# Feature-map attention and a gated convolution on one core: two alternating phases become one hand-ordered pipeline of 36 units

## The chip, the cores and the metric

The kernel runs on one core of one Trainium2 chip. The metric is the device time of one execution in microseconds (us). The core's engines are PE (TensorE, with its weight loads shown apart as PEld), DVE (VectorE), ACT (ScalarE), POOL (GpSimd) and SP (SyncE, which here only issues DMAs). Each works through its own queue in order and waits on semaphores for the others.

## The reference

Eight batches, eight heads, 576 tokens, head dimension 64, 128 features, all inputs float32:

```python
def phi(x):                                   # q, k: (8, 8, 576, 64); w_phi: (64, 128)
    proj = np.einsum('bhsd,df->bhsf', x, w_phi)
    proj = proj - np.max(np.abs(proj), axis=-1, keepdims=True)
    return np.concatenate([np.exp(proj), np.exp(-proj)], axis=-1)
q_p, k_p = phi(q), phi(k)
kv = np.einsum('bhsf,bhsd->bhfd', k_p, v)
z = np.sum(k_p, axis=2)
num = np.einsum('bhsf,bhfd->bhsd', q_p, kv)
den = np.einsum('bhsf,bhf->bhs', q_p, z)[..., None] + 1e-06
x = (num / den)                               # heads side by side: (8, 576, 512)
gate = sigmoid(causal depthwise conv of x, 5 taps, conv_w (5, 512))
out = (gate * (x @ w_val)) @ w_out            # (8, 576, 512)
```

## The kernel before

A batch's tokens are cut into five chunks, four of 128 and one of 64 that is padded to 128 (`CHUNKS`). Matmul operands are bf16; POOL's DMAs convert while they load. A batch passes through these steps:

- Loads (L110, L111, L119): 15 DMAs per batch from POOL, one for each chunk of q, k and v, in runs of 64 floats (256 B).
- `emit_transposes` (L136): PE transposes q and k of two heads at a time into PSUM (L142, L153), DVE copies them to QT2 and KT2 (L147 to L159).
- `emit_qmax` (L163): q is projected with tokens on the partitions (five matmuls, 640 columns) only so that DVE can take the largest magnitude per token (L171). `emit_mqrows` turns these maxima into rows (L182, L183).
- `emit_kproj` (L185): k is projected the same way into PK; DVE takes the maxima (L194), ACT writes exp(PK) and exp(-PK) to KTIL (L198, L199).
- `emit_vscale` (L201): ACT takes exp of minus and plus the k maxima (EMK, EPK, L204, L205); POOL multiplies v by them (L211) and puts them in an extra 65th column (L215). That column gives z.
- `emit_qproj` (L219): q is projected with features on the partitions into PQ; the q maxima are subtracted by matmuls with EB (L224, L226); ACT writes both exps to QTIL (L227, L228).
- KV (L388): 10 matmuls of 65 columns per head, evacuated by DVE (L248).
- `emit_num` (L253): per chunk 16 matmuls of 65 columns (L259), then DVE's reciprocal and product (RCP L268, XN L270). `emit_xtp` (L278) transposes XN on PE and copies it to XT on DVE (L283, L284): here the heads of all channels come to the partitions.
- The MLP: per 256 tokens and 128 channels four matmuls with WVAL (L292) and five with diagonal matrices of the taps, DIAG (L300), which are the convolution; tanh on ACT (L307; the sigmoid is 0.5 (1 + tanh(x/2)), with the halves folded into weights), the gated product on DVE (L310); then matmuls with WOUT (L322), a copy on ACT (L329) and the store from SP (L330).

The outer loop alternates two phases, each with its own PSUM pools. `phase_X` does transposes, maxima and k of batch i+1 together with the MLP of batch i-2, and ends with `emit_vscale`; `phase_Y` does q and KV of batch i together with NUM and XTP of batch i-1. The code gives a program order, and a scheduler then chooses the order in each engine's queue. The half-size contraction of 64 is padded: W4 holds w_phi in 64 of 128 rows and zeros in the others, so every such matmul is a full one.

Of the kernel before, what the change touches and what calls it, by code (L numbers as in the profile page):

```python
# [10 lines left out]
ALU = mybir.AluOpType  # L11

# [5 lines left out]
NF = 2 * F  # L18
DM = 512
P = 128  # L20
CHUNKS = [(0, 128), (128, 128), (256, 128), (384, 128), (512, 64)]
NCH = len(CHUNKS)
TOKPAD = 4
QCOLS = 640


class _BatchState:
    pass


@with_exitstack
def kernel(
# [11 lines left out]
    nc = tc.nc  # L44

    const = ctx.enter_context(tc.tile_pool(name="const", bufs=1))

    ident_bf = const.tile([P, P], BF16, name="ident_bf")
    make_identity(nc, ident_bf[:])
    ident_f = const.tile([P, P], FP32, name="ident_f")  # L50
    make_identity(nc, ident_f[:])
# [3 lines left out]
    nc.sync.dma_start(wtmp[D:2 * D, :], w_phi[:, :])  # L55
    W4 = const.tile([P, 2, NF], BF16, name="W4")
    nc.vector.memset(W4[:, :, :], 0.0)
    nc.vector.tensor_copy(W4[0:D, 0, 0:F], wtmp[0:D, :])
    nc.vector.tensor_scalar_mul(W4[0:D, 0, F:NF], wtmp[0:D, :], -1.0)
    nc.vector.tensor_copy(W4[D:2 * D, 1, 0:F], wtmp[D:2 * D, :])  # L60
    nc.vector.tensor_scalar_mul(W4[D:2 * D, 1, F:NF], wtmp[D:2 * D, :], -1.0)

    EB = const.tile([P, H, P], BF16, name="EB")
    for h in range(H):
        nc.vector.tensor_copy(EB[:, h, :], ident_f[:, h:h + 1].to_broadcast([P, P]))

    WVAL = const.tile([P, 4, DM], BF16, name="WVAL")
    nc.gpsimd.dma_start(WVAL[:, :, :], moe_w_val.rearrange("(dt p) j -> p dt j", p=P))
    WOUT = const.tile([P, 4, DM], BF16, name="WOUT")
    nc.gpsimd.dma_start(WOUT[:, :, :], moe_w_out.rearrange("(jt p) o -> p jt o", p=P))  # L70
    nc.vector.tensor_scalar_mul(WOUT[:, :, :], WOUT[:, :, :], 0.5)

    cw5 = const.tile([5, DM], FP32, name="cw5")
    nc.sync.dma_start(cw5[:, :], moe_conv_w[:, :])
    cwT = const.tile([P, 4, 5], FP32, name="cwT")
    with tc.tile_pool(name="ps_cw", bufs=1, space=bass.MemoryType.PSUM) as ps_cw:
        cwps = ps_cw.tile([P, 4, 5], FP32, name="cwps")
        for dt in range(4):
            nc.tensor.transpose(cwps[:, dt, :], cw5[:, dt * P:(dt + 1) * P], ident_f[0:5, 0:5])
        nc.vector.tensor_copy(cwT[:, :, :], cwps[:, :, :])  # L80
    DIAG = const.tile([P, 4, 5, P], BF16, name="DIAG")
    cwTh = const.tile([P, 4, 5], FP32, name="cwTh")
    nc.vector.tensor_scalar_mul(cwTh[:, :, :], cwT[:, :, :], 0.5)
    for dt in range(4):
        for tap in range(5):
            nc.vector.tensor_scalar_mul(DIAG[:, dt, tap, :], ident_f[:, :], cwTh[:, dt, tap:tap + 1])

    qkp = ctx.enter_context(tc.tile_pool(name="qkp", bufs=3))
    vnp = ctx.enter_context(tc.tile_pool(name="vnp", bufs=2))
    xtp = ctx.enter_context(tc.tile_pool(name="xtp", bufs=2))  # L90
    qtp = ctx.enter_context(tc.tile_pool(name="qtp", bufs=8))
    ktp = ctx.enter_context(tc.tile_pool(name="ktp", bufs=4))
    featq = ctx.enter_context(tc.tile_pool(name="featq", bufs=2))
    featk = ctx.enter_context(tc.tile_pool(name="featk", bufs=2))
    smallp = ctx.enter_context(tc.tile_pool(name="smallp", bufs=2))
    vtp = ctx.enter_context(tc.tile_pool(name="vtp", bufs=1))
    kvp = ctx.enter_context(tc.tile_pool(name="kvp", bufs=2))
    xnp = ctx.enter_context(tc.tile_pool(name="xnp", bufs=3))
    mlp_sb = ctx.enter_context(tc.tile_pool(name="mlp_sb", bufs=2))

    def load_qk(st):
        bi = st.bi
        st.QN = qkp.tile([P, NCH, H, D], BF16, name="QN")
        st.KN = qkp.tile([P, NCH, H, D], BF16, name="KN")
        nc.gpsimd.memset(st.QN[64:P, NCH - 1, :, :], 0.0)
        nc.gpsimd.memset(st.KN[64:P, NCH - 1, :, :], 0.0)
        qrb = q[bi].rearrange("h s d -> s h d")
        krb = k[bi].rearrange("h s d -> s h d")
        for c, (s0, sz) in enumerate(CHUNKS):
            nc.gpsimd.dma_start(st.QN[:sz, c, :, :], qrb[s0:s0 + sz])  # L110
            nc.gpsimd.dma_start(st.KN[:sz, c, :, :], krb[s0:s0 + sz])  # L111

    def load_v(st):
        bi = st.bi
        st.VN = vnp.tile([P, NCH, H, D], BF16, name="VN")
        nc.gpsimd.memset(st.VN[64:P, NCH - 1, :, :], 0.0)
        vrb = v[bi].rearrange("h s d -> s h d")
        for c, (s0, sz) in enumerate(CHUNKS):
            nc.gpsimd.dma_start(st.VN[:sz, c, :, :], vrb[s0:s0 + sz])  # L119

    def alloc_A(st):
        st.MQ = smallp.tile([P, H, NCH], FP32, name="MQ")
        st.MK = smallp.tile([P, H, NCH], FP32, name="MK")
        st.MQR = smallp.tile([P, S], BF16, name="MQR")
        st.KTIL = featk.tile([P, H, NCH, NF], BF16, name="KTIL")
        st.QT2 = []
        st.KT2 = []
        st.VTs = []

    def alloc_Q(st):  # L130
        st.QTIL = featq.tile([P, H, 2, QCOLS], BF16, name="QTIL")
        nc.gpsimd.memset(st.QTIL[:, :, :, S:QCOLS], 1.0)
        st.KVSB = kvp.tile([P, H, 2, D + 1], BF16, name="KVSB")
        st.XN = {}

    def emit_transposes(st, hp, psX):  # L136
        QT2 = qtp.tile([P, 640], BF16, name="QT2")
        KT2 = ktp.tile([P, 640], BF16, name="KT2")
        srcs = ((st.QN, QT2, 0), (st.KN, KT2, 1))
        T2 = psX.tile([P, 2, 128], BF16, name="T2")  # L140
        for src, dst, ti in srcs:
            nc.tensor.transpose(  # L142
                T2[:, ti, 0:P],
                src[:, 4, 2 * hp:2 * hp + 2, :].rearrange("p h d -> p (h d)"),
                ident_bf[:, :],
            )
        nc.vector.tensor_copy(QT2[:, 512:640], T2[:, 0, 0:128])  # L147
        nc.vector.tensor_copy(KT2[:, 512:640], T2[:, 1, 0:128])
        T = psX.tile([P, 2, 512], BF16, name="T", tag="T")
        for c in range(4):  # L150
            s0, sz = CHUNKS[c]
            for src, dst, ti in srcs:
                nc.tensor.transpose(  # L153
                    T[:, ti, s0:s0 + sz],
                    src[:, c, 2 * hp:2 * hp + 2, :].rearrange("p h d -> p (h d)"),
                    ident_bf[:, :],
                )
        nc.vector.tensor_copy(QT2[:, 0:512], T[:, 0, :])
        nc.vector.tensor_copy(KT2[:, 0:512], T[:, 1, :])  # L159
        st.QT2.append(QT2)  # L160
        st.KT2.append(KT2)

    def emit_qmax(st, h, psX):  # L163
        hp, h2 = h // 2, h % 2
        PQA = psX.tile([P, NCH, F], FP32, name="PQA", tag="PA", bufs=2)
        for c, (s0, sz) in enumerate(CHUNKS):
            nc.tensor.matmul(  # L167
                PQA[:, c, :], st.QT2[hp][:, s0:s0 + P], W4[:, h2, 0:F],
                start=True, stop=True,
            )  # L170
        nc.vector.tensor_reduce(  # L171
            st.MQ[:, h, :], PQA[:, :, :],
            mybir.AxisListType.X, ALU.max, apply_absolute_value=True,
        )

    def emit_mqrows(st, psX):
        MQT = psX.tile([P, 640], BF16, name="MQT", tag="T")
        MQb = smallp.tile([P, NCH, P], BF16, name="MQb")
        nc.vector.memset(MQb[:, :, :], 0.0)
        nc.vector.tensor_copy(MQb[:, :, 0:H], st.MQ[:, :, :].rearrange("p h c -> p c h"))  # L180
        for c, (s0, sz) in enumerate(CHUNKS):
            nc.tensor.transpose(MQT[:, s0:s0 + P], MQb[:, c, :], ident_bf[:, :])  # L182
        nc.vector.tensor_scalar_mul(st.MQR[:, :], MQT[:, 0:S], -1.0)  # L183

    def emit_kproj(st, h, psX):  # L185
        hp, h2 = h // 2, h % 2
        KT2 = st.KT2[hp]
        PK = psX.tile([P, NCH, F], FP32, name="PK", tag="PA", bufs=2)
        for c, (s0, sz) in enumerate(CHUNKS):
            nc.tensor.matmul(  # L190
                PK[:, c, :], KT2[:, s0:s0 + P], W4[:, h2, 0:F],
                start=True, stop=True,
            )
        nc.vector.tensor_reduce(  # L194
            st.MK[:, h, :], PK[:, :, :],
            mybir.AxisListType.X, ALU.max, apply_absolute_value=True,
        )
# [31 lines left out]

    KVBLK_PER_PASS = 7  # L230

    def emit_kv(st, h, KVPS):
        for ft in range(2):
            VT = st.VTs[ft]
            blk = h * 2 + ft
# [248 lines left out]
```

## Time and profile before

| what | value |
|---|---|
| three runs | 414.79, 416.35, 417.25 us; median 416.35 |
| span of the profiled execution, first to last instruction | 414.7 us |
| instructions in it | 8908 |
| mean granted PE clock (1 is full speed) | 0.892 |
| DMAs issued by POOL for q, k, v | 120, 0.91 us of POOL each |
| longest sums of waits | ACT's tanh for L300's matmuls 99.6 us; DVE's RCP for L259's 54.5 us; ACT's first exp of k for L194's maxima 47.6 us |

The profile gives each engine's busy time and instruction count. A matmul's duration includes its way through the array, so matmuls overlap and the distance from start to start is the cost of one in a row; the chain of work that ended last shows such distances. In the windows answer a row holds PE, PEld, DVE, ACT and POOL busy time with the number of instructions, then the granted PE clock, the DMA engines' share and GB/s.

### The profile page before, as it was taken

The page shows a single profiled execution, that of the slowest core. Times are in us where ns is not written, and L with a number is a line of the kernel's source. Part 1 is how long each engine was busy: PE and PEld are TensorE (multiplying, and loading weights), DVE is VectorE, ACT ScalarE, POOL GpSimd, SP SyncE. Part 2 cuts the span into 40 slices and gives each one's busy share as a digit, 9 for nine tenths or more (in the row PEclk, how much of TensorE's full clock was granted, in tenths as well). Part 3 has the DMA queues.
Part 4 walks back from the last instruction along what each step waited for, and adds up shares of the span by engine and source line. Part 5 has one row for each costly group of instructions (what it writes and reads, how often), then busy time and mean ns, then how long its engine had stood idle before and what let it go on. Part 6 is the DMA issues. An engine that isn't in the chain of part 4 may idle for free.

```text
span 414.7 us, 8908 instructions
## 1 busy us (share of the span) xinstructions
PE 310.2 (75%) x3685; PEld 231.5 (56%) x3724; DVE 239.8 (58%) x564; ACT 206.4 (50%) x409; POOL 200.6 (48%) x210
## 2 busy tenths in 40 slices
PE   0285656764989598959798779877987798797595
PEld 0164544553777367737684568656854565574462
DVE  7386682593569657953687357846882622622421
ACT  1007248528713981497238743794377535633033
POOL 9899799999099309930850068005400360000000
PEclk9999965965889999997898789999996989989589
DMA  7999699929409900990091006500110011011011
GB/s 110 152 132 133 41 64 112 112 15 129 31 2 142 144 3 2 138 149 2 3 107 54 13 2 47 115 14 2 52 52 13 3 51 66 2 52 63 2 52 64
DMA packets 119028, 25.30 MB, mean 61 GB/s; under 512 B 113222, under 2 KB 114374, under 8 KB 118987
## 3 DMA queue, kind: packets, MB, share of 16 engines
q0 software_dynamic: 113568, 15.21, 58.0%
q1 hardware_dynamic: 5418, 9.52, 6.6%
q8 instruction: 29, 0.48, 0.5%
q14 instruction: 13, 0.10, 0.1%
HBM read 30.48 MB, written 9.44 MB: 96 GB/s over the span
## 4 chain that ended last, share of the span: by engine, by line
PE 50%; DVE 21%; ACT 19%; issue 4%; DMA 4%; POOL 0%; ACTq 0%; DVEq 0%; POOLq 0%
ACT KTIL L199 8%; PE VG L300 8%; PE VG L292 7%; DVE MQ L171 7%; ACT KTIL L198 6%; PE NUM L259 6%; PE OUTp L322 5%; PE KVPS L388 5%; PE PQ L223 4%; PE T L153 4%; PE PQA L167 3%; DVE MK L194 3%; DVE XN L270 3%; DVE XT L284 3%; PE PQ L224 2%
## 5 line engine op out<-in xcount | busy, mean ns | idle before, releaser
L307 ACT ACTIVATE GATEs<-VG 128x256 bf16<-128x256 f32 (+1 forms) x96 | 32.5, 351 | 106.6 <-PE VG L300 99.6
L198 ACT ACTIVATE KTIL<-PK 128x640 bf16<-128x640 f32 x64 | 46.4, 724 | 59.5 <-DVE MK L194 47.6
L194 DVE TENSOR_REDUCE MK<-PK 128x5 f32<-128x640 f32 x64 | 52.7, 824 | 20.5 <-PE PK L190 20.3
L300 PE MATMUL VG<-XT,DIAG 128*128 128x256 bf16 (+1 forms) x480 | 59.7, 257 | 0.0
L310 DVE SCALAR_TENSOR_TENSOR GV<-GATEs,VG 128x256 bf16<-128x256 bf16 (+1 forms) x96 | 33.3, 352 | 41.5 <-ACT GATEs L307 40.8
L292 PE MATMUL VG<-XT,WVAL 128*128 128x256 bf16 (+1 forms) x384 | 53.6, 258 | 3.4 <-ACT OUTs L329 1.3
L171 DVE TENSOR_REDUCE MQ<-PQA 128x5 f32<-128x640 f32 x64 | 50.8, 819 | 5.1 <-PE PQA L167 4.8
L227 ACT ACTIVATE QTIL<-PQ 128x576 bf16<-128x576 f32 x64 | 42.1, 658 | 18.7 <-PE PQ L226 18.3
L199 ACT ACTIVATE KTIL<-PK 128x640 bf16<-128x640 f32 x64 | 46.4, 725 | 0.0
L322 PE MATMUL OUTp<-WOUT,GV 128*128 128x512 bf16 (+1 forms) x144 | 41.8, 389 | 2.8 <-DVE GV L310 2.0
L300 PEld LDWEIGHTS <-DIAG 128*128 128x128 bf16 x480 | 39.9, 102 | 5.9
L228 ACT ACTIVATE QTIL<-PQ 128x576 bf16<-128x576 f32 x64 | 42.1, 657 | 0.0
L268 DVE RECIPROCAL RCP<-NUM 128x8 f32<-128x8 f32 x40 | 8.2, 206 | 54.5 <-PE NUM L259 54.5
L292 PEld LDWEIGHTS <-WVAL 128*128 128x128 bf16 x384 | 32.7, 101 | 11.0 <-issue 4.0
L259 PE MATMUL NUM<-KVSB,QTIL 128*128 128x65 bf16 x640 | 30.1, 203 | 10.5 <-DVE XN L270 9.7
L111 POOL DMA_DIRECT2D KN<-in_k_dram x40 | 36.3, 909 | 1.6 <-DMA WOUT<-in_moe_w_out_dram 1.2
L110 POOL DMA_DIRECT2D QN<-in_q_dram x40 | 36.2, 905 | 0.0
L119 POOL DMA_DIRECT2D VN<-in_v_dram x40 | 34.3, 914 | 0.0
L259 PEld LDWEIGHTS <-QTIL 128*128 128x128 bf16 x640 | 25.6, 104 | 15.0 <-DVE XN L270 14.1
L329 ACT ACTIVATE OUTs<-OUTp 128x512 f32<-128x512 f32 (+1 forms) x40 | 24.1, 601 | 19.3 <-PE OUTp L322 19.3
L153 PE MATMUL T<-ident_bf,QN 128*128 128x128 bf16 x128 | 21.9, 247 | 10.5 <-DMA QN<-in_q_dram 10.0
L388 PEld LDWEIGHTS <-KTIL 128*128 128x128 bf16 x640 | 28.2, 105 | 1.6 <-issue 1.5
(500 smaller groups left out, 611.1 us busy)
## 6 DMA issues: line engine op xcount, KB each, us to landing
out_dram<-OUTs SPq DMA_DIRECT2D x32, 256.0 KB, 2.0
QN<-in_q_dram POOLq DMA_DIRECT2D x32, 128.0 KB, 5.6
KN<-in_k_dram POOLq DMA_DIRECT2D x32, 128.0 KB, 5.6
VN<-in_v_dram POOLq DMA_DIRECT2D x32, 128.0 KB, 4.4
out_dram<-OUTs SPq DMA_DIRECT2D x8, 128.0 KB, 2.3
WVAL<-in_moe_w_val_dram POOLq DMA_DIRECT2D x1, 512.0 KB, 6.1
WOUT<-in_moe_w_out_dram POOLq DMA_DIRECT2D x1, 512.0 KB, 9.0
QN<-in_q_dram POOLq DMA_DIRECT2D x8, 64.0 KB, 5.8
```

Source lines behind the costliest of these rows:

```text
L153: nc.tensor.transpose(T[:, ti, s0:s0 + sz], src[:, c, 2 * hp:2 * hp + 2, :].rearrange("p h d -> p (h d)"), ident_bf[:, :],)
L171: nc.vector.tensor_reduce(st.MQ[:, h, :], PQA[:, :, :], mybir.AxisListType.X, ALU.max, apply_absolute_value=True,)
L194: nc.vector.tensor_reduce(st.MK[:, h, :], PK[:, :, :], mybir.AxisListType.X, ALU.max, apply_absolute_value=True,)
L198: nc.scalar.activation(st.KTIL[:, h, :, 0:F], PK[:, :, :], AF.Exp, scale=1.0)
L199: nc.scalar.activation(st.KTIL[:, h, :, F:NF], PK[:, :, :], AF.Exp, scale=-1.0)
L227: nc.scalar.activation(st.QTIL[:, h, 0, 0:S], PQ[:, :], AF.Exp, scale=1.0)
L228: nc.scalar.activation(st.QTIL[:, h, 1, 0:S], PQ[:, :], AF.Exp, scale=-1.0)
L259: nc.tensor.matmul(NUM[:, g, hh * 65:(hh + 1) * 65], st.QTIL[:, h, ft, s0:s0 + P], st.KVSB[:, h, ft, :], start=(ft == 0), stop=(ft == 1),)
L292: nc.tensor.matmul(VG[:, 0, 0:tsz], WVAL[:, dt, jt * P:(jt + 1) * P], XT[:, dt, TOKPAD + t0:TOKPAD + t0 + tsz], start=(dt == 0), stop=(dt ...
L300: nc.tensor.matmul(VG[:, 1, 0:tsz], DIAG[:, jt, tap, :], XT[:, jt, cs:cs + tsz], start=(tap == 0), stop=(tap == 4),)
L322: nc.tensor.matmul(OUTp[0:subsz, :], GVs[jt][:, sub:sub + subsz], WOUT[:, jt, :], start=(jt == 0), stop=(jt == 3),)
L388: nc.tensor.matmul(KVPS[:, col:col + 65], stq.KTIL[:, h, c, ft * F:(ft + 1) * F], stq.VTs[ft][:, c, h, :], start=(c == 0), stop=(c == NCH ...
```

## The change

The kernel is written anew. What it does:

- **Tokens.** The first 512 tokens of a batch are loaded with four neighbours in one partition, so that runs are 1 KB for q, k and v, one DMA per tensor and batch. The last 64 tokens of two batches form one tail tile of 128 partitions.
- **Units.** A group of two batches is nine units: one tail unit (all eight heads, 64 tokens of each of the two batches), then four head pairs of 512 tokens for each batch. All 36 units have the same shapes: 1024 columns of k and of q features per partition.
- **One loop.** Step s works on unit s, with KV of unit s-1 and NUM of s-1 or of a tail, the transposes of s+2, and one MLP part of an older batch: a gate part, a value part or the tail part. The loop runs 48 steps, all inside `tc.manual_schedule()`, where the order written is that of each queue.
- **PSUM** is five fixed slots with one buffer each: A (k projection), B (PQ, later NUM), C (q for the maxima, later gate, val, tail), D (transposes, later KV and the turned maxima), E (outputs).
- **Half-array matmuls.** Contractions of 64 run on 64 rows of the array, upper and lower alternately, without zero rows; the convolution uses 64 x 64 diagonal blocks in four quarters of the array.
- **Scaling of v** is done per unit: DVE's maxima, negation on POOL, exp on ACT (op_E), product and cast on POOL (op_V).
- **Heads to partitions.** XTP on PE and its copy on DVE are replaced by SP's `dma_start_transpose` from XN to XT. Since tokens are strided, a tap shift is another j or, across the partition run, a shift by one column of XT; the tail gets its four earlier tokens by a small POOL copy (op_halo).
- **In the excerpt below** op_KV is 20 matmuls of 65 columns for a pair unit, op_MQT turns the q maxima into rows, op_KVM copies KV and these rows to SBUF on DVE, op_shift subtracts the maxima in PSUM, and op_gate has 8 parts of 4 quarters, five taps of 512 columns in all.
- **Output copies** run on ACT in val steps, otherwise on DVE.

The diff, cut to its core:

```diff
+    def load_main(name, src, b, h0=0, h1=H):
...
+        nc.gpsimd.dma_start(t[:, h0:h1, :],
+            src[b, h0:h1, 0:SM, :].rearrange("h (p j) d -> p h (j d)", j=4))
...
+    def tokproj(ps, u, i):
+        for blk in range(4):
+            for rg in range(2):
+                r = slice(rg * 64, rg * 64 + 64)
+                nc.tensor.matmul(ps[:, rg, blk * P:(blk + 1) * P], u.T[r, i, blk, :], W2[r, :],
+                    start=True, stop=True)
...
+    def op_neg(u):
+        nc.gpsimd.tensor_scalar_mul(u.MK[:, 0, :], u.MK[:, 1, :], -1.0)
+    def op_E(u):
+        u.E = smallp.tile([P, 2, 8], FP32, name="E")
+        nc.scalar.activation(u.E[:, :, :], u.MK[:, :, :], AF.Exp)
...
+    def op_V(u):
...
+            nc.gpsimd.tensor_tensor(dst[r, :, :, 0:D],
+                src[r].unsqueeze(1).to_broadcast([n, 2, 8, D]),
+                u.E[r].unsqueeze(3).to_broadcast([n, 2, 8, D]), ALU.mult)
+            nc.gpsimd.tensor_copy(dst[r, :, :, D:E1], u.E[r].unsqueeze(3))
...
+    def op_X(u):
+        if not u.tail:
+            nc.sync.dma_start_transpose(XTs[u.b % 2][:, u.hp, :, 16:PL],
+                u.XN[:, :, :, :].rearrange("p a x d -> p (a x d)"))
...
+    def quarters(q2):
+        for par in range(2):
+            for rg in range(2):
+                cg = rg if par == 0 else 1 - rg
+                yield 2 * q2 + par, slice(rg * 64, rg * 64 + 64), slice(cg * 64, cg * 64 + 64), par
+    def op_gate(m, q2):
+        ps = slot2("C")
...
+        for n, (dl, j0, j1) in enumerate(parts):
+            for dt, r, c, par in quarters(q2):
...
+                nc.tensor.matmul(ps[c, par, j0 * P:j1 * P], DIAG[r, dt, 4 - dl, :], mv,
+                    start=(n == 0), stop=(n == len(parts) - 1), skip_group_check=True)
...
+        for s in range(NS):
+            u, u1, u2 = U(s), U(s + 1), U(s + 2)
+            p1, p2 = U(s - 1), U(s - 2)
...
+            if u is not None:
+                op_maxQ(u)
+            if u is not None or p1 is not None:
+                op_KV(p1, u)
+            if u is not None:
+                op_MQT(u)
+            x = num_of(s - 2)
+            if x is not None:
+                op_XN(x)
+                op_X(x)
+            if kind == "gate":
+                op_gate(m, q2)
+            elif kind == "val":
+                op_val(m, q2, 0)
+            elif kind == "tail":
+                op_tailgv(m)
+            if u is not None or (p1 is not None and not p1.tail):
+                op_KVM(p1, u)
+            if u is not None:
+                op_PK(u)
+                op_PQ(u)
+                op_shift(u)
+            if kind == "gate":
+                op_tanh(m, q2)
...
+            elif kind == "val":
+                op_val(m, q2, 1)
+            if u is not None:
+                op_maxK(u)
+                op_neg(u)
+                op_Qexp(u, 0)
+                op_Qexp(u, 1)
+                op_Kexp(u, 0)
+                op_E(u)
+                op_Kexp(u, 1)
+                op_V(u)
+            for f in loads.get(s, []):
+                f()
+            if kind == "val":
+                op_GV(m, q2)
...
+            if u2 is not None:
+                op_T(u2)
+                op_Tcopy(u2)
+            if om is not None:
+                op_out(*om)
+                op_outev(*om, "act" if kind == "val" else "dve")
+                if om[1] in (None, 1, 3):
+                    op_store(*om)
+            x = num_of(s - 1)
+            if x is not None:
+                op_NUM(x)
+            if u1 is not None:
+                op_PQA(u1)
...
```

Gate and value parts of a batch follow three steps after its last unit, in the order gate, val, gate, val, and its outputs from the seventh step on, one per step. Before the loop DVE zeroes the tiles that keep zero halves (QZ, VZ, the first columns of XT) and builds SEL and the identities.

More of the change, by code (lines that the diff above doesn't have):

```diff
@@ new lines @@
+    units = []
+    for G in range(B // 2):
+        for kind in range(9):
+            u = _U()
+            u.G = G
+            u.tail = kind == 0
+            u.b = None if u.tail else 2 * G + (kind - 1) // 4
+            u.hp = None if u.tail else (kind - 1) % 4
+            u.idx = len(units)
+            units.append(u)
+    NU = len(units)
+    pair_of = {(u.b, u.hp): u for u in units if not u.tail}
+    tail_of = {u.G: u for u in units if u.tail}
+    main = {}
+    tails = {}
+    def load_main(name, src, b, h0=0, h1=H):
+        if (name, b) not in main:
+            t = loadp.tile([P, H, 4 * D], BF16, name=name + "N")
+            main[name, b] = t
+        t = main[name, b]
+        nc.gpsimd.dma_start(
+            t[:, h0:h1, :],
+            src[b, h0:h1, 0:SM, :].rearrange("h (p j) d -> p h (j d)", j=4),
+        )
@@ L59 @@
[L59 to L68, printed above, removed]
@@ L78, with load_weights @@
+    WVtmp = const.tile([P, 4, 2, P], BF16, name="WVtmp")
+    def load_weights():
+        wv = moe_w_val.rearrange("(dt p) (q two c) -> p dt q two c", p=P, two=2, c=P)
         for dt in range(4):
[L79 to L83, printed above, removed]
@@ L113, in load_v @@
[L113 to L128, printed above, removed]
@@ new lines, in col, with op_T @@
+    def col(u, name, blk):
+        if u.tail:
+            return tails[name, u.G][:, 2 * blk:2 * blk + 2, :].rearrange("p h d -> p (h d)")
+        t = main[name, u.b]
+        return t[:, 2 * u.hp + blk // 2, (blk % 2) * P:(blk % 2 + 1) * P]
+    def op_T(u):
+        u.Tps = psum.tile([P, 2, 4, P], BF16, name="Tps", tag="D")
+        for i, name in enumerate(("k", "q")):
+            for blk in range(4):
+                nc.tensor.transpose(u.Tps[:, i, blk, :], col(u, name, blk), ident_bf[:, :])
@@ new lines, in op_MQT, with op_KVM @@
+    def op_MQT(u):
+        nc.tensor.matmul(
+            u.kvps[:, 4 * E1:4 * E1 + P], u.MQb[:, :, :].rearrange("p r c -> p (r c)"),
+            ident_bf[:, :], start=True, stop=True,
+        )
+    def op_KVM(ukv, umq):
+        t = kvp.tile([P, 4 * E1 + P], BF16, name="KVM")
+        haskv = ukv is not None and not ukv.tail
+        lo = 0 if haskv else 4 * E1
+        hi = 4 * E1 + P if umq is not None else 4 * E1
+        ps = umq.kvps if umq is not None else ukv.kvps2
+        nc.vector.tensor_copy(t[:, lo:hi], ps[:, lo:hi])
+        if haskv:
+            ukv.KVS = t
+        if umq is not None:
+            umq.MQR = t
@@ L176, in emit_mqrows @@
[L176 to L192, printed above, removed]
-            )
-        nc.vector.tensor_reduce(
-            st.MK[:, h, :], PK[:, :, :],
-            mybir.AxisListType.X, ALU.max, apply_absolute_value=True,
-        )
-        nc.scalar.activation(st.KTIL[:, h, :, 0:F], PK[:, :, :], AF.Exp, scale=1.0)
-        nc.scalar.activation(st.KTIL[:, h, :, F:NF], PK[:, :, :], AF.Exp, scale=-1.0)
@@ new lines, in op_store @@
+    def op_store(m, j):
+        if j is None:
+            for bb in range(2):
+                nc.sync.dma_start(out[2 * m.G + bb, SM:S, :], m.OS[bb * ST:(bb + 1) * ST, :])
+        else:
+            ov = out[m.b, 0:SM, :].rearrange("(p j) o -> p j o", j=4)
+            nc.sync.dma_start(ov[:, j - 1:j + 1, :], m.OS[:, j - 1:j + 1, :])
+    mlps = []
+    bt = {}
+    ot = {}
+    for b in range(B):
+        m = M()
+        m.b = b
+        m.GATE = {}
+        last = pair_of[b, 3].idx
+        s0 = last + 3
+        for q2 in range(2):
+            bt[s0 + 2 * q2] = ("gate", m, q2)
+            bt[s0 + 2 * q2 + 1] = ("val", m, q2)
+        for j in range(4):
+            ot[s0 + 4 + j] = (m, j)
+        mlps.append(m)
```

693 lines of the change are left out of this document (388 added, 305 removed).

## The prediction

> **What bounds the kernel now.** I read the busy shares first, then the chain of work that ended last. No engine is full: PE, the fullest, has 75% of the span, DVE 58%, ACT 50%.
>
> ```profile
> span 414.7 us, 8908 instructions
> ...
> PE 310.2 (75%) x3685; PEld 231.5 (56%) x3724; DVE 239.8 (58%) x564; ACT 206.4 (50%) x409; POOL 200.6 (48%) x210
> ...
> PE 50%; DVE 21%; ACT 19%; issue 4%; DMA 4%; POOL 0%; ACTq 0%; DVEq 0%; POOLq 0%
> ```
>
> The chain hops: half of it is PE, a fifth each DVE and ACT. Phase X holds DVE (L171, L194) and ACT (L198, L199) to the ends of their rows, phase Y holds PE, and neither fills the other's gaps. So what bounds it is the alternation, and the new kernel must be priced by its own loop, not by busy sums. Pieces of the chain give the rates for that:
>
> ```profile
> 184.73 0.59 ACT KTIL L198
> 185.32 0.60 ACT KTIL L199
> ...
> 195.71 0.22 PE PQ L223
> ...
> 196.19 0.30 PE KVPS L388 x10
> ```
>
> Columns: start, duration until the next piece, what. ACT starts a 640-column exp every 0.59, that is 0.53 for the columns (QTIL's 576 columns at 0.657 and OUTs' 512 at 0.605 give 0.83 ns each) and 0.06 beside them. PE at full clock takes 0.215 for 512 columns, hence 0.056 for 128, and 0.030 for 65 columns with a fresh stationary of 128 each: weight loads hide. The third rate is POOL's:
>
> ```profile
> L211 POOL TENSOR_TENSOR VT_1836<-VN,EMK x1: 4541/4541/4541, 155.2 to 155.2; 128x2560 bf16<-128x2560 bf16 x1
> ...
> L215 POOL CAST VT_1836<-EMK x1: 357/357/357, 159.6 to 159.6; 128x40 bf16<-128x40 f32 x1
> ```
>
> The product takes 1.77 ns an element, and the cast of the E column 0.36.
>
> **Work by engine.** The new DVE has per unit two reductions of 1024 columns. From L171 (0.819 for 640, so 0.15 and 1.04 ns a column) one is 1.22, and 1.14 where they follow each other. With the bf16 copy of 1024 (L158: 0.42 for 512, so 0.69), the cast of 388 (L248: 0.63 for 455, so 0.56), RCP 0.21 and XN 0.61 that is 4.3; GV (two of 1.22 a batch) and half of the output copies make it 5.1 a step. ACT: four exps of 1024 at 0.91 to 0.95, E, tanh, output copies: 4.5. PE: KV 0.61, MQT 0.06, T 0.45, out 0.86, NUM 0.52, and PQA, PK, PQ and shift 0.9 to 1.8, so 3.4 to 4.3, and 1 to 3 of MLP. Thirty-six steps at 5.1 would be 184. The loop is longer.
>
> **The loop of one step.** Everything below is in the order in which each queue holds it. Zero is the end of op_shift of one unit.
> 1. PE's last result to ACT: 0.20 (L226's mean 204 ns).
> 2. Qexp0, Qexp1, Kexp0 stand ahead of E in ACT's queue: 3 x 0.95 = 2.85 (0.91 by the row above; some pieces of L198 and L199 are 0.75 to 0.81 where PE runs, so I take a little more).
> 3. E: 0.24 (L204, 40 columns).
> 4. op_V on POOL waits for E: 1024 x 1.77 = 1.82, and the cast 0.36: 2.18.
> 5. The next step's op_KV waits for this VT: 20 matmuls x 0.030 and MQT 0.06: 0.66.
> 6. Four hops at 0.05 ("issue" pieces of the chain): 0.20. So far 6.33.
> 7. On PE behind MQT: op_gate or op_val, then PK, PQ, shift. Only then does ACT start again.
>
> That op_maxK, op_neg, op_XN and op_KVM are not late: maxK ends about 0.9 after zero, E is wanted at 3.05; XN ends near 5.4, PQ is wanted after 6.3; KVM (0.56 behind MQT) fits beside the gate. POOL's DMA issues (0.91 each, up to three a step) stand behind op_V and end before the next op_neg is wanted; if not, E is late by the rest. They are 48 against 120, with 1 KB runs for q, k, v main in place of 256 B.
>
> **Half-array matmuls** are what the trace of before cannot price. PK, PQ and shift have 64 rows and alternate between the upper and lower half; the gate has 64 x 64 quarters, 20 full-width quarters of 512 columns for each op_gate. Serial: PK 8 x 0.056, PQ 2 x 0.215, shift 8 x 0.056: 1.33; gate 20 x 0.215 = 4.3. All overlapped: 0.66 and 1.07. The nearest row is L322's 64-column stationary (418 ns mean, no faster than 128 columns), but there one half follows itself. Starts are spaced by the columns that stream in (0.22) while a single 128-column matmul lasts 0.31, so the entry of the rows is what is shared; halves with other rows don't share it. I take rows overlapped and columns not: 0.66, and 2.13 for the gate. The skill's page TensorE: Matmul & The Clock Gate, Part 3, says that tiles in different row groups run at once, 3.07 times as fast for four of 32 rows; by it, with all four quarters at once, the sum below would be 17 lower. Against it, the page TensorEngine Tiling (Array Packing) of the Trainium skill, Key Properties, says that a change of tiling mode drains the array, and this order changes it two to four times a step. No run here shows either yet.
>
> **The sum.** A gate step is 6.33 + 2.13 + 0.66 + 0.25 (tanh stands ahead of the next Qexp0) = 9.37; a val step 6.33 + 4 x 0.215 + 0.66 = 7.85; a step without MLP 6.33, KVM 0.2 + 0.56, shift 0.25 = 7.36. Behind a tail unit op_KV does nothing, and the B slot decides: PQA at 3.1, maxQ 1.2, XN 0.9, PQ and shift: 6.3. Steps 1 to 35 hold 4 behind tails (25), 5 without MLP (37), 16 with gate or tail MLP (150; the tail's 40 small and 16 full matmuls are 2.0), 10 with val (78): 290.
>
> Start: DVE's constants queue ahead of the first Tcopy. The identity comes after four tail loads on POOL (4 x 0.7, to 4.2), then SEL and identities 1.2, four zeroings of 1088 words at 1.02 ns (L179's row) 4.6, VZ and XT 2.5: 12.5. Tcopy twice, PQA, maxQ, KVM, shift at a cold clock: 17.5 (first loads land under it; now the first transpose waits until 12.5). End, after the last unit's shift: V and KV 6, gate 1.5, NUM and XN 2.5, crossbar about 3, then four gate and val steps of b7 alone at about 3 each, tail MLP 3, five outputs that share one PSUM bank at 1.9, last store 2.0 to 2.3: 43 with some cold matmuls. Together 17.5 + 290 + 43 = 351. The page's span is 414.7 and the median of the runs 416.35, so 1.65 lies around it: **353**. I add 2 for waits of several semaphores: **355**, 15% below before.
>
> **The crossbar** has no row before. Between below nothing (16 XTP transposes and XT copies a batch leave PE and DVE: 17.8 and 15.8 of busy time) and a wait of a whole step. XN ends at 5.4 of a step, the gate that reads it starts at 6.3 of the next: 9 of slack. The nearest rows are the stores (2.0 from issue to landing for 256 KB) and the 256-byte loads (5.6); both fit. I take nothing inside the loop, and 3 once at the end.
>
> **Rivals.**
> - Half-array matmuls run one after another: gate steps +2.17, all others and these +0.67, end +8: 355 + 16 x 2.17 + 31 x 0.67 + 8 = 418. That is the same time or a little more. Chance 0.17.
> - **The PE clock falls in the loop's gaps** (ends slower). In each step PE has T and out (1.3), waits for Qexp1 until 2.2, does NUM and PQA until 3.1, and waits for V until 5.5. The windows of before show what a gap does:
>
> ```profile
> 228.00:230.00 2.00, 1.09 (x6) 0.45 (x5) 1.57 (x2) 1.52 (x3) 0.00 (x0) 0.71 0.00 0
> 230.00:232.00 2.00, 0.47 (x5) 0.38 (x7) 0.00 (x0) 1.67 (x5) 0.00 (x0) 1.00 0.29 66
> 232.00:234.00 2.00, 2.00 (x36) 1.66 (x36) 0.00 (x0) 1.77 (x4) 0.00 (x0) 0.65 0.00 0
> 234.00:236.00 2.00, 2.00 (x25) 1.45 (x23) 0.90 (x2) 0.96 (x2) 0.00 (x0) 0.50 0.00 0
> ```
>
>   (PE busy is the second figure, the granted clock the third from the end.) After 2 us with 0.47 of PE the clock is at half for some 4 us. The new loop's gap of 2.3 is about as long, but with NUM and PQA before it. Always at half, the loop pays its PE part again: 3.45 on gate steps, 2.2 on val steps, 1.6 on others, 55 + 22 + 14, and 10 at the end: 455. From two thirds of the steps it is slower than before. The Trainium skill's page TensorE: Matmul & The Clock Gate, Part 1, says that an idle window of about 3.4 us halves the clock; by that rule alone a gap of 2.3 would cost nothing and the sum would stay. The trace is stricter: L223's longest wait, the one that ends at 231.5, was 2.4, and the half clock followed. What speaks against the rival: windows whose bursts come every 1.3 us (220 to 226, PE busy 1.2 to 1.5 of 2) kept the full clock. Chance 0.12 for over 385.
> - The loop isn't what I think, V or E early, and DVE bounds: 36 x 5.6 and 60: 262. Against it: the code's order puts E behind three exps. Chance 0.06.
> - The crossbar lands later than 9: every batch's gate waits, at 12 a transpose 36 x 12 + 40 = 470. Chance 0.07.
>
> **Numbers.** Forecast 0.58 (315 to 390). Low end: full overlap -17, start and end -10, V and exps a little shorter: 318. High end takes in serial halves: 425. Within 0.5% is about what a measurement can't tell from no change. Faster 0.73 (forecast, DVE-bound, half of the serial case, part of a late crossbar and a sagging clock), same 0.04, slower 0.23.
>
> **What would show it.** Steps of about 8.5 on average; POOL's V ending just before KV in the chain, with ACT the largest share and POOL no longer 0%; PE idle by E or V some 2 us a step; gate of 32 matmuls in about 2; granted clock above 0.85; DVE near 200 of busy time and below 65%. The prediction is wrong if the chain runs through DVE or the crossbar, if a gate takes over 4, or if the clock is below 0.7.

## The result, and the profile after

The new kernel takes 359.45 us (median of four runs, 359.05 to 360.06) against 416.8 (414.79 to 417.78). The ratio is 0.863, with an interval of 0.860 to 0.866. The forecast was 355 with a range of 315 to 425. It came within 4.5 us, and below it is shown that this closeness is owed to errors that cancel.

The page of the new kernel: span, busy shares, granted PE clock in 40 slices, shares of the chain of work that ended last, and the group of POOL's product.

```profile
span 357.6 us, 8222 instructions
...
PE 236.4 (66%) x3552; PEld 157.0 (44%) x3552; DVE 204.9 (57%) x278; ACT 166.0 (46%) x215; POOL 144.5 (40%) x195
...
PEclk9975656566998988989898988988998998889998
...
PE 35%; ACT 23%; POOL 20%; issue 15%; DVE 5%; DMA 1%; SPq 0%; ACTq 0%; POOLq 0%; DVEq 0%
...
L278 POOL TENSOR_TENSOR VT<-vN,E 128x1024 bf16<-128x1024 bf16 x32 | 60.9, 1902 | 61.3 <-ACT E L257 61.3
```

Every engine has less to do than before (PE 74 us less, DVE 35, ACT 40, POOL 56), yet none is fuller: PE has 66% of the span where it had 75%. POOL, which had 0% of the chain, has 20%, and the product has 61.3 us of waiting for E in front of it. The mean clock is lower, 0.852 against 0.892.

One gate step in the chain of waits, at full clock (start, duration until the next piece, what):

```profile
179.61 0.91 ACT QTIL L358
...
180.53 1.02 ACT QTIL L358
181.55 0.92 ACT KTIL L262
182.47 0.11 ACT E L257
182.57 0.07 issue
182.65 1.90 POOL VT L278
184.55 0.21 POOL VT L283
...
185.65 1.25 PE psC L452 x32
...
186.92 1.02 ACT GATE L459
187.94 0.64 ACT QTIL L358
```

This is the loop that the prediction wrote down, in the same order. Three exps stand ahead of E (2.86 from 179.61 to 182.47), then E and its hop, POOL's product and cast, KV and the turned maxima from 184.80 to 185.65 (0.85), the gate, the tanh, and the next first exp. Counted to the next step's first exp, a step of this kind takes 8.23. The waits say the same over the whole span (total, times, longest):

```profile
PE KVps L299 <- POOL VT L283: 70.6, 31, 6.3
...
POOL VT L278 <- ACT E L257: 61.3, 32, 2.3
```

**Where the clock goes.** The windows of that step and of the value step after it (PE, PEld, DVE, ACT, POOL busy, granted clock, DMA share, GB/s):

```profile
180.60:182.60 2.00, 2.00 (x42) 1.53 (x40) 1.82 (x2) 2.00 (x5) 1.18 (x3) 1.00 0.13 18
182.60:184.80 2.20, 0.55 (x16) 0.41 (x13) 1.58 (x3) 1.37 (x2) 2.15 (x3) 1.00 1.13 134
184.80:187.90 3.10, 3.10 (x77) 2.29 (x77) 1.60 (x3) 0.98 (x2) 0.80 (x1) 1.00 1.03 177
188.90:190.90 2.00, 1.13 (x25) 0.84 (x24) 0.94 (x3) 2.00 (x4) 0.03 (x1) 1.00 1.94 87
190.90:193.10 2.20, 0.08 (x3) 0.08 (x3) 1.98 (x3) 0.80 (x1) 2.20 (x3) 1.00 0.76 110
193.10:196.90 3.80, 3.80 (x44) 2.03 (x44) 1.33 (x2) 0.00 (x0) 1.41 (x3) 0.60 0.79 69
```

In both steps PE waits while POOL multiplies, for 1.65 us in the first and 2.22 in the second. In the first, PE was busy throughout the 2 us before the wait and 0.55 in the next 2.20, and the clock stays at 1.00. In the second it was busy 1.13 of 2.00 and then 0.08 of 2.20, and the work behind it runs at 0.60. PE holds less work there: in the first step the rest of a value part, the transposes, an output and the 32 NUM matmuls of a tail unit, in the second only the 16 of a pair unit, a q projection and the end of an output, done early.

That alone doesn't decide it. Every change of the granted clock in this trace falls on a grid of 3.41 us, and so do those of the kernel before and of the experiments. The clock fell at 19 points of this grid, with PE busy for 0.98 to 1.76 of the 3.41 us just before; at 50 points it stayed full, with PE busy for 1.49 or more; and it came back only behind 3.10 or more. Two value steps, those behind the first exps at 205.14 and 282.76, have the same pieces up to V and a wait of the same length, but the grid cuts them differently. The rows are two neighbouring grid cells for each:

```profile
207.51:210.92 3.41, 1.19 (x37) 1.06 (x33) 2.03 (x3) 1.49 (x3) 2.75 (x3) 1.00 1.01 92
210.92:214.33 3.41, 3.41 (x31) 1.55 (x27) 1.26 (x2) 0.00 (x0) 0.21 (x1) 0.50 0.81 109
...
286.01:289.42 3.41, 1.48 (x25) 0.98 (x24) 2.34 (x4) 0.61 (x1) 1.87 (x2) 1.00 0.15 29
289.42:292.84 3.42, 3.42 (x46) 2.10 (x45) 2.57 (x3) 2.32 (x3) 0.23 (x1) 1.00 0.32 21
```

The first wait lies within one cell (PE busy 1.19), and half clock follows. The second is cut at 286.01, its cell has 1.48 of PE, and the clock stays. So which steps are hit is in part chance: step 9 takes 8.23 here and 9.53 in the experiment that spreads the weight loads, and the four runs of this kernel have mean clocks of 0.852 to 0.876. The matmuls behind the wait show the price. In the first of the two value steps,

```profile
211.27 1.71 PE psC L467 x4
212.97 0.54 PE psA L224 x7
213.51 0.43 PE psB L332 x2
213.94 0.45 PE psB L341 x7
```

are 3.13 us of PE, where the same four groups take 1.65 at full clock (the experiment with PE kept busy shows them).

**By class of step** (distance from first exp to first exp, in the trace):

| part | predicted | measured |
|---|---|---|
| start, to the first exp | 17.5 | 18.0 |
| 4 steps behind a tail unit | 25 | 23.4 |
| 5 steps without MLP | 37 | 45.1 |
| 13 gate and 3 tail steps | 150 (9.37 each) | 145.8: six gate steps 8.22 or 8.23, seven 9.39 to 10.22; tails 8.60, 10.05, 10.08 |
| 10 value steps | 78 (7.85 each) | 86.7: three 7.71 to 7.77, seven 8.63 to 9.75 |
| steps 1 to 35 | 290 | 301.0 |
| end, from the last unit's first exp | 43 | 38.6 |

Of the steps without MLP one, step 4, is 12.1 long; the others are 8.0 (three) and 8.9. The chain there goes through POOL's queue:

```profile
36.68 0.20 POOL VT L283
...
38.22 0.70 POOL WVAL L175
...
45.62 0.59 POOL WOUT L180
46.21 0.29 POOL MK L253
...
46.52 0.22 ACT E L257
```

Twelve weight loads, written into step 2, hold POOL from 38.2 to 46.2. The negation of the k maxima (MK, L253) stands behind them, and E behind that.

### The profile page after: what moved, and what is told of

It is laid out like the page before. It is cut to its first block, busy times and chain, and to the rows that moved or that the text cites. A ratio compares the mean times of both kernels' runs of the same rounds, so it can differ in the third digit from the quotient of the medians.

```text
span 357.6 us, 8222 instructions
## 1 busy us (share of the span) xinstructions
PE 236.4 (66%) x3552; PEld 157.0 (44%) x3552; DVE 204.9 (57%) x278; ACT 166.0 (46%) x215; POOL 144.5 (40%) x195
## 4 chain that ended last, share of the span: by engine, by line
PE 35%; ACT 23%; POOL 20%; issue 15%; DVE 5%; DMA 1%; SPq 0%; ACTq 0%; POOLq 0%; DVEq 0%
POOL VT L278 13%; ACT QTIL L358 12%; ACT KTIL L262 7%; PE psC L452 6%; PE KVps L299 6%; PE psC L467 6%; PE psA L224 3%; PE psB L341 3%; PE psB L332 3%; PE OUTps L519 2%; POOL VT L283 2%; ACT GATE L459 2%; PE psC L496 2%; ACT QZ L354 1%; PE KVps L304 1%
## 5 line engine op out<-in xcount | busy, mean ns | idle before, releaser
L358 ACT ACTIVATE QTIL<-psB 128x1024 bf16<-128x1024 f32 x64 | 62.0, 1021 | 79.8 <-PE psB L341 79.8
L278 POOL TENSOR_TENSOR VT<-vN,E 128x1024 bf16<-128x1024 bf16 x32 | 60.9, 1902 | 61.3 <-ACT E L257 61.3
L299 PE MATMUL KVps<-VT,KTIL 128*128 128x65 bf16 x512 | 27.9, 206 | 72.7 <-POOL VT L283 70.6
L246 DVE TENSOR_REDUCE MK<-psA 128x8 f32<-128x1024 f32 x36 | 44.1, 1225 | 44.4 <-PE psA L224 44.2
L262 ACT ACTIVATE KTIL<-psA 128x1024 bf16<-128x1024 f32 x64 | 65.4, 1035 | 0.0
L239 DVE TENSOR_REDUCE MQb<-psC 128x8 bf16<-128x1024 f32 x36 | 44.0, 1223 | 29.0 <-PE psC L224 28.9
L253 POOL TENSOR_SCALAR MK<-MK 128x8 f32<-128x8 f32 x36 | 8.6, 240 | 103.8 <-DVE MK L246 85.7
L467 PE MATMUL psC<-XT,WVAL 128*128 128x512 bf16 x128 | 39.1, 440 | 0.3 <-ACT GATE L459 0.3
L519 PE MATMUL OUTps<-WOUT,GV 128*128 128x512 bf16 x128 | 32.9, 379 | 2.7 <-DVE OS L530 2.7
L224 PEld LDWEIGHTS <-T 64*128 64x128 bf16 x576 | 19.5, 106 | 24.8 <-issue 16.6
L452 PE MATMUL psC<-XT,DIAG 64*64 64x384 bf16 (+3 forms) x512 | 27.0, 365 | 0.5 <-DVE GV L475 0.5
L400 DVE TENSOR_TENSOR XN<-psB,RCP 128x512 bf16<-128x512 f32 x36 | 24.9, 691 | 1.2
L224 PE MATMUL psA<-W,T 64*128 64x128 bf16 x288 | 18.7, 268 | 0.8 <-ACT KTt L262 0.8
```

The lines of the kernel that those rows point to most:

```text
L224: nc.tensor.matmul(ps[:, rg, blk * P:(blk + 1) * P], u.T[r, i, blk, :], W2[r, :], start=True, stop=True,)
L239: nc.vector.tensor_reduce(u.MQb[:, :, 0:4], u.PQA[:, :, :].rearrange("p r (b f) -> p r b f", f=F), AX.X, ALU.max, apply_absolute_value=True,)
L246: nc.vector.tensor_reduce(u.MK[:, 1, :].rearrange("p (b r) -> p r b", r=2), u.PK[:, :, :].rearrange("p r (b f) -> p r b f", f=F), AX.X, AL ...
L262: nc.scalar.activation(u.KT[:, ft, :, :, :].rearrange("p r b f -> p r (b f)"), u.PK[:, :, :], AF.Exp, scale=1.0 if ft == 0 else -1.0,)
L278: nc.gpsimd.tensor_tensor(dst[r, :, :, 0:D], src[r].unsqueeze(1).to_broadcast([n, 2, 8, D]), u.E[r].unsqueeze(3).to_broadcast([n, 2, 8, D] ...
L299: nc.tensor.matmul(o, ukv.KT[:, ft, rg, h2 * 2 + j2, :], ukv.VT[:, ft, (h2 * 2 + j2) * 2 + rg, :], start=(c == 0), stop=False,)
```

## The experiments

All were timed beside the kernel before on the same chips (its medians there: 416.45, 416.72 and 417.02). Theory: a loop over four queues, exps, E, POOL's product, KV, MLP, sets the step, with a half clock wherever PE's wait is long and bare. Rivals: DVE is the bound; the crossbar holds the gates; the half-array matmuls do not overlap.

### POOL's product twice

```diff
     op_V:
+            nc.gpsimd.tensor_tensor(dst[r, :, :, 0:D], ..., ALU.mult)
             nc.gpsimd.tensor_tensor(dst[r, :, :, 0:D], ..., ALU.mult)
```

> POOL's product of v and E runs twice in each unit (the second writes the same values again). Loop theory (E on ACT, product on POOL, KV on PE are one chain in every step): the 31 steps behind a pair unit grow by the 1.90 us that one product takes, 359.5 + 31 x 1.9 = 418 us. Rival, DVE's 57% of busy time or the sum of work per engine sets the pace: POOL has 40% busy and room, 360 to 365 us. Rival, PE is the bound: 360 to 365 us.

Measured: 462.03 us, ratio 1.110 (1.107 to 1.113), 102.6 more than the new kernel. The product is on the loop: 31 of them at 1.90 are 59. The other 44 have three sources. About 17 lie in steps 2, 11, 20 and 29, which take 14.3 to 15.8 where their neighbours take 10.0 to 12.3: a tail unit has two products, the edit doubles both, and POOL comes late to the negation of the next unit's maxima. The end is 4.5 longer. The remaining 22 or so are left for PE's clock. Chain of this kernel in a gate step:

```profile
257.38 1.92 POOL VT L278
...
259.37 1.90 POOL VT L283
...
262.37 2.05 PE psC L457 x32
264.42 0.54 PE psA L224 x8
264.96 0.43 PE psB L337 x2
265.38 0.44 PE psB L346 x8
```

With a wait of over 4 us PE is at half clock behind it: the gate takes 2.05 in place of 1.25 and the three groups behind it 1.41 in place of 0.79. So a step that had full clock and loses it by a longer wait pays about 1.4 more in PE time. The expectation had only the 1.90.

### DVE's copy of T twice

```diff
     op_Tcopy:
+        nc.vector.tensor_copy(u.T[:, :, :, :], u.Tps[:, :, :, :])
         nc.vector.tensor_copy(u.T[:, :, :, :], u.Tps[:, :, :, :])
```

> DVE's copy of the transposes (0.68 us, 0.60 from start to start) runs twice in each unit. Loop theory: it falls into DVE's idle time, 360 to 363 us. Rival, DVE sets the pace: 36 x 0.6 = 22 us more, 381 us.

Measured: 361.49, ratio 0.868 (0.865 to 0.872). Some 23 us more of DVE's busy time (227.8 against 204.9) cost 2, all of it ahead of the first exp (20.1 in place of 18.0). The rival that DVE is the bound falls.

### E ahead of two exps

```diff
                 op_Qexp(u, 0)
+                op_E(u)
                 op_Qexp(u, 1)
                 op_Kexp(u, 0)
-                op_E(u)
                 op_Kexp(u, 1)
```

> ACT takes op_E directly behind Qexp0 instead of behind Kexp0; nothing else moves. Loop theory: E then waits for DVE's k maxima and their negation, which end 0.1 to 0.9 us behind Qexp0's start plus its 0.91, so V starts 1.65 to 1.85 us earlier; KV and the turning of the q maxima then wait for DVE's maxQ at 1.5 to 1.6 us earlier than now. 31 x 1.5 = 46 us less, and PE's gap shrinks, so that the half clock on val steps (about 1.4 us on 10 steps) may go too: 300 to 315 us. Rival, DVE or the sum of work: 355 to 362 us.

Measured: 305.07, ratio 0.734 (0.730 to 0.738): 54.4 us less for the place of one instruction of 0.23 us. Value steps take 6.48 or 6.49, gate steps 7.04 to 7.65, and the clock is 0.953. In this piece of its chain KV follows ACT's last exp and not POOL:

```profile
199.38 0.92 ACT KTIL L262
...
200.35 0.30 PE KVps L299 x4
```

POOL's waits for E fall from 61.3 to 11.2, and KV's for POOL from 70.6 to 9.7. The 54 are two effects. Set against the same steps at full clock (gate 8.23, tail 8.60, value 7.7), the 26 steps with MLP behind pair units are 30 shorter in all, 1.0 to 1.3 each. Another 22 are what the half clock had cost these steps before. The two exps taken out of the loop are 1.94 a step, so something else came to bound it after 1.0 to 1.3; what that is was not separated. The chain is now spread over PE 26%, POOL 25%, ACT 18%.

### Halves and quarters one after another

In tokproj, the shift and the taps the loop over the halves (quarters) becomes the outer one, so that neighbours share their part of the array. The count and size of the matmuls stay.

```diff
-        for n, (dl, j0, j1) in enumerate(parts):
-            for dt, r, c, par in quarters(q2):
+        for dt, r, c, par in quarters(q2):
+            for n, (dl, j0, j1) in enumerate(parts):
```

> The same matmuls, but those that use one half (PK, the q projection for the maxima, shift) or one quarter of the array (gate, tail taps) follow each other instead of alternating. If the overlap of halves and quarters is what makes a gate 1.25 us: gate 20 x 0.215 = 4.3 us, 16 x 3 = 48 us more; PK and shift 0.21 us more each on 31 steps, 13 us; together 420 us, less what a warmer PE clock gives back on val steps (up to 14), so 405 to 420. Rival, the quarters don't overlap and the gate is short for another reason: 360 us.

Measured: 407.09, ratio 0.977 (0.973 to 0.982), 47.6 more than the new kernel. Two gates in its chain:

```profile
203.65 4.56 PE psC L452 x26
...
315.03 2.95 PE psC L452 x26
```

The first ran at a granted clock of 0.62, the second at 1.00, so it is the second that may be set beside the 1.25 above: in a row the same matmuls take 2.4 times as long. At full clock a gate step is 9.93 in place of 8.23; 1.7 for 16 steps is 27 of the 47.6. The end is 9 longer. Eleven of the 16 gates ran at 0.61 to 0.67, where seven of the new kernel's ran below full clock.

So the overlap is real, and the records of the new kernel show that all four quarters share, not the rows alone: their matmuls start 2 to 5 ns apart, four at a time. A strict row of 20 x 0.215 = 4.3 came about in neither order: even here a new quarter begins every 0.57 us, while its five taps of 512 columns need 1.08. That the rival's 418 lies near the 407 is therefore not a confirmation of its price; it had the full clock and 4.3 for a gate.

### PE kept busy while it waits

Thirty-six matmuls of 124 columns, into unused columns of the D slot, in PE's queue ahead of op_KV.

```diff
     op_KV:
+            for i in range(36):
+                nc.tensor.matmul(ps[:, 388:512], ident_bf[:, :], umq.T[:, 0, i % 4, 0:124],
+                                 start=True, stop=True, skip_group_check=True)
```

> 36 extra matmuls of 124 columns ahead of op_KV in each step write columns of the D bank that nobody reads; PE so has work while it waits for V. They take 1.9 us at full clock and the gap is 1.7 to 2.4. Clock theory (the gap makes PE's clock fall, and a val step then runs at half clock): granted clock 0.95 or more, val steps 1.4 us shorter on some 10 steps and the steps before the MLP begins 1 us shorter, 335 to 348 us. Rival, the clock has another cause or the loop doesn't feel it: 359 us or, where the extra work delays KV, up to 375.

Measured: 339.5, ratio 0.812 (0.804 to 0.820), clock 0.978. More work on PE, 277.7 busy in place of 236.4, and 20 us less time. A value step in its chain:

```profile
199.84 0.86 PE psC L471 x4
200.70 0.33 PE psA L224 x8
201.03 0.22 PE psB L336 x2
201.25 0.24 PE psB L345 x8
```

These are the groups that took 3.13 above. Value steps now take 7.70 to 7.77, gate steps 8.22 to 8.47, tail steps 8.60: the new kernel's own steps where it has full clock. In these steps 22 us are won, and 2 in those without MLP; the steps behind a tail unit are 3 longer and the end 1. So filling the wait wins back 20 us net, and the half clock costs the new kernel somewhat more than that.

### No crossbar

> The crossbar transposes are left out, and the MLP works on tiles of zeros, which the start writes once: heads are not brought to the partitions. Prediction's reading (9 us of slack in the loop, a wait of some us at most at the end): 354 to 361 us, about 1 us of it for the larger zeroing at the start. Rival, the crossbar or its queue holds back a step or a batch: 8 batches x 2 us or more, under 345 us. Zeros in the MLP may also draw less current; a change of the granted clock would show that.

Here SP's transposes into XT and XH are left out, and the MLP works on zeros. Measured: 363.81, ratio 0.868 (0.861 to 0.876): not faster, 4 above the new kernel. DVE's zeroing of XT and XH puts the first exp at 20.8 in place of 18.0, where 1 us had been expected; that is 2.8 of the 4. From the first to the last unit's first exp it takes 300.9, against 301.0, and the steps at full clock are alike (gate 8.22 or 8.23, value 7.71 to 7.77): in the loop the crossbar holds nothing. The rival of a late crossbar falls.

### The weight loads spread

Two of the twelve loads in each of steps 1 to 6, what needs them in step 7.

```diff
-    add_load(2, load_weights)
-    add_load(4, finish_weights)
+    for part in range(6):
+        add_load(1 + part, lambda part=part: load_weights(part))
+    add_load(7, finish_weights)
```

> The 12 weight loads, which POOL issues in a row in step 2, are issued two a step in steps 1 to 6. In the trace they hold POOL from 38.2 to 46.2 and op_neg of the next unit behind them, so that this step takes 12.1 us where its neighbours take 8.0 to 8.1. Theory: 4 us less, 355 to 356 us. Rival, the ramp is bound by the first loads' landing: 359 us.

Measured: 356.1, ratio 0.851 (0.845 to 0.858), 3.35 less. Step 4 takes 8.05 in place of 12.1. So the queue behind the loads was the cause; it costs 4.05 in that step, of which 3.35 reach the end.

### The MLP moved out of the loop

E early, loads spread; gate, value and tail matmuls behind op_shift, so that they run while ACT does the exps; tanh behind E; PQA ahead of NUM.

```diff
-            if kind == "gate":
-                op_gate(m, q2)
...
                 op_shift(u)
+            if kind == "gate":
+                op_gate(m, q2)
...
                 op_Qexp(u, 0)
+                op_E(u)
+            if kind == "gate":
+                op_tanh(m, q2)
...
                 op_Qexp(u, 1)
```

> op_E directly behind Qexp0, the MLP's gate, val and tail matmuls behind op_shift instead of ahead of PK, tanh behind E, PQA ahead of NUM, and the weight loads spread. The MLP then lies beside the exps, outside the loop: Qexp0, E, V or the q maxima, KV, KVM, shift. A step is then about 6.0 to 6.4 us, near DVE's 5.1 and PE's 5: 36 x 6.2 + 18 + 38 = 279, so 270 to 290 us. If E alone was the gain and PE is what binds after it: 300 to 305 us, as with E early alone.

Measured: 290.48 (287.46 to 291.53), ratio 0.693 (0.686 to 0.700), the lowest time of all. It is just above the top of what was expected. Against E early alone it is 14.6 less, but 8.7 of this lie in steps 2 to 6, which have no MLP (step 4 falls from 12.5 to 5.6, as the loads are spread). Gate and tail steps are 0.3 and 0.8 shorter on average, value steps 0.4 longer: once E is early, the MLP's place gains little in them. What it and PQA's place do was not run apart. Its busy shares, and a value step in its chain:

```profile
PE 223.4 (77%) x3552; PEld 143.9 (50%) x3552; DVE 200.0 (69%) x278; ACT 167.9 (58%) x215; POOL 144.5 (50%) x195
```

```profile
157.05 0.57 DVE KVM L322
...
157.67 0.40 PE psB L341 x8
158.07 1.85 PE psC L467 x8
...
160.01 1.23 DVE GV L475
...
161.28 0.40 PE psC L224 x8
```

In a value step PE and DVE now hand work back and forth. The gated product GV waits for all eight matmuls of L467, and the next q projection (L224) waits for GV, because both use slot C. Gate steps still go through ACT, which has 24% of the chain; PE has 28% and DVE 21%.

### The same order with E in its old place

> As the kernel with the MLP behind op_shift, but op_E again behind Kexp0. Loop theory: zero is shift's end; Qexp0, tanh on gate steps, Qexp1 and Kexp0 until 3.0 or 3.9, E and V 2.4, KV 0.6, turned maxima and KVM 0.8, shift 0.4: 7.2 on val steps and steps without MLP, 8.1 on gate steps; 35 steps of 7.5, 18.5 for the start and 36 for the end: 310 to 325 us. Rival, in that order E's place no longer counts, since DVE or PE binds: 288 to 294 us.

Measured: 338.82, ratio 0.811 (0.805 to 0.817). Expected was 310 to 325, so the size is missed: steps average 8.0 where 7.5 was taken, and the clock is 0.906, not 0.968. The direction stands. In this order too E's place is worth 48 us, and the rival, that E's place no longer counts there, falls. Against the loads spread alone (356.1) the MLP's and PQA's new places are worth 17 while E is late.

### GV in two halves

GV as one instruction for each of the two PSUM banks, so that the first could start after four of the eight matmuls.

> As the kernel with the MLP behind op_shift and E early, but the gated product GV is two DVE instructions, one for each bank, so that the first starts while the second half of val runs. In the trace a val step's chain is val 1.85, GV 1.23, PQA, NUM, RCP, XN, KVM, shift. Theory: GV ends 0.5 to 0.6 us earlier on 16 val steps, 8 to 10 us less, 280 to 284 us. Rival, DVE's own queue binds (69% busy, and the split adds 0.15 us a val step): 290 to 293 us.

Measured: 291.63 (291.07 to 294.20), ratio 0.701 (0.695 to 0.707), no gain where 8 to 10 us were expected. DVE's timeline of this kernel shows why the theory wasn't put to the test:

```profile
159.93 1.28 DVE L476 SCALAR_TENSOR_TENSOR GV<-GATE,psC 128x512 bf16<-128x512 bf16 x2 [1.26 <-PE psC L467]
```

The first half starts at 159.93, after the last of the eight matmuls, with DVE idle for 1.26 before it, and the second follows at once. So the early start never came about. Why the first half waits for both banks stays open.

## Why the prediction was right, and where not

**The mechanism was right.** The loop of exps, E, V, KV, MLP was read from the order of the queues, and it is what the chain shows, in most pieces to the size: 2.86 for the exps (2.85 predicted), 1.90 and 0.21 for POOL (1.82 and 0.36), 0.85 for KV and the maxima (0.66). PE's wait for V, which the prediction had as some 2 us a step, is 70.6 in 31 waits, 2.3 each. Doubling V and moving E confirm it from both sides. One of its signs failed: ACT was to have the largest share of the chain, and it has 23% where PE has 35%. The clock was to be above 0.85, and 0.852 only just is.

**The gate was mis-sized: 2.13 against 1.25.** The prediction took rows as overlapping and columns as not, and all four quarters overlap. The row that it argued from mixes two clocks: the 0.31 of a 128-column matmul stands in a stretch at half clock, and at full clock one lasts 0.22. The Trainium skill's page TensorE: Matmul & The Clock Gate, Part 3, has row tiles at once with 3.07 times for four; the trace agrees in kind, with 1.25 for what would be 4.3 at 0.215 for each quarter of 512 columns, one after another. The drain at a change of mode, from the Trainium skill's page TensorEngine Tiling (Array Packing), Key Properties, doesn't show: 20 quarters of 512 columns, four at a time, are 5 x 0.215 = 1.08 of streaming, and the gate's 32 matmuls take 1.25 in the chain. At full clock a gate step is 8.23 in place of 9.37; 0.88 of this difference is the gate, the rest lies in hops and KV. A tail step is 8.60. Over the 16 steps that were counted at 9.37 this is 17 us, which the prediction had given as what full overlap would take off.

**The clock was not in the sum.** It was a rival (455 at half clock throughout; 0.12 for over 385), and it came in part: seven of 13 gate steps, two of three tail steps and seven of 10 value steps are 0.9 to 2.0 longer than the rest of their kind, 22 us in all, and the steps without MLP have some 4.5 more. Filling the wait gave 20 us back, a fifth of the 100 between 355 and 455. The clock and the gate cancel in large part, and that they do is luck. The argument against the rival, that bursts every 1.3 us kept the clock in the kernel before, did not carry over: between 188.9 and 193.1 above there are 4.2 us with 1.2 of PE. It was also misread, since the last of its three windows (224 to 226) has a granted clock of 0.94: half clock began at 225.8, behind 2.08 of PE in 3.41 us. By the Trainium skill's TensorE: Matmul & The Clock Gate, Part 1, it takes an idle window of about 3.4 us. The trace agrees with the length, the 3.41 of its grid, but such a window need not be idle: the clock fell behind cells with up to 1.76 of PE, and a single wait of 2.2 us was enough.

**"Up to three a step" was wrong.** Step 2 issues 12 weight loads on POOL, and the prediction counted only q, k and v. Spreading them took 3.35 off.

**Steps without MLP:** 8.0, and not 7.36, apart from step 4 and the first. The granted clock is 0.5 to 0.6 in that stretch (fourth to eighth of the 40 slices above); the term assumed full clock. With PE kept busy three of these steps take 7.13 to 7.19.

**The end:** 38.6 against 43. The same overlap makes the gates of the last batch shorter than taken; how much of the 4.4 is due to that was not tried.

**The crossbar** was put at nothing within the loop, with 9 of slack; the trace has it land at 4.2 (median; 2.4 to 7.0) for the pairs, and leaving it out changes the loop by 0.1:

```profile
XT<-XN SPq DMA_TRANSPOSE x32, 4.2
...
XH<-XN SPq DMA_TRANSPOSE x8, 6.6
```

**DVE** has 204.9 busy at 57%, as predicted (near 200, under 65%), and it is not the bound. The case "V or E early" that was dismissed as against the code's order is what the third experiment then made: 305, where the rival had 262. DVE alone was not what came next: it has 8% of that chain.

So the sum, 290 for steps 1 to 35 against 301, holds errors of about -17 (gate and tail steps), +27 (clock, with and without MLP) and +4 (weight loads), -3 is in smaller ones, and the end is 4 shorter. The time within 1.3% is not a measure of how well each term was known.

## What to carry to other kernels

In an order written by hand, write down the loop that goes through all queues, and price that, not the busy sums: where it runs through a small instruction, that instruction's place decides. Here 0.23 us of E behind two exps cost 54 us of 359, some 22 of them by way of the clock. Put what the loop doesn't need (here the MLP) beside it, on an engine while it waits; with PQA's new place that was worth 17 us with E late and little with E early. Ask of every wait on PE whether it also costs the clock: filling it, with real or with idle work, is worth measuring. And compare two matmul times only at the same granted clock.

## What the runs showed of the hardware

- PE's granted clock changed only on a grid of 3.41 us, in the new kernel, the one before and the experiments. In the new kernel it fell to half behind cells in which PE was busy for 0.98 to 1.76 us (in the one before up to 2.08), held behind 1.49 or more, and came back behind 3.10 or more. Between 1.49 and 1.76 both happened, so no sharp boundary is shown. Dummy matmuls in the wait brought the mean clock from 0.852 to 0.978.
- At full clock, four quarters of 64 by 64 taken in turn ran 2.4 times as fast as in a row (1.25 against 2.95 for the same 32 matmuls), with no visible cost of changing over from full-array matmuls.
- POOL's product of 1024 bf16 with two broadcast operands took 1.90 us in every kernel, and the issue of a 64 KB weight load held POOL for 0.70.
